# First attention layer: output weights fetched from ScalarE's queue, den steps one to an output unit, scale chain in four parts

## The chip, the cores and the metric

One NeuronCore of a Trainium2 chip runs the whole program. The metric is device time in microseconds (us) of one execution, lower is better. Each result below is a set of executions. One execution, of the set or beside it, is recorded by the hardware profiler, and its *span* is about 1.9 us shorter than its device time. Every execution also reports the mean clock that TensorE was granted (1.0 is full speed). "Fast" is what the records call all the runs compared.

## The reference, cut to what matters

Four residual layers on a 2048 x 1024 bf16 input: attention, gated unit, attention, gated unit, each behind a layer norm.

```python
# attention layer (1st and 3rd), H = 32 heads of 32
q, k, v = split(layernorm(x) @ wqkv)
pq, pk  = phi(q), phi(k)                  # phi(t) = t+1 if t>0 else exp(t), plus 1e-6
kv      = einsum("bhsd,bhse->bhde", pk, v)
den     = einsum("bhqd,bhd->bhq", pq, pk.sum(s)) + 1e-6
x       = x + (pq @ kv / den) @ wo
# gated layer (2nd and 4th)
x       = x + ((layernorm(x) @ w_gate) * (layernorm(x) @ w_up)) @ w_down
```

## The kernel before: what the change and the argument touch

The program is scheduled by hand: each engine executes its instructions in the order in which the Python code emits them. An attention layer goes: k units, key products (`xk`), twelve q units mixed with key products, a `kv` unit, four more q units mixed with eight key-value-output units (`kvo_unit`, the first users of `wo`), then 16 output units (`out_tile`). The first layer also does work for the second: it scans all gated-layer weights (`scans`, a Square with an accumulator on ScalarE), turns the sums into power-of-two scales (the scale chain), and prepares the first down weights (`dp`).

```python
wo = [ST[:]..., TX[:, 0:HEAD]...]        # the two halves of the output weights; ST, TX held normalised rows

def load_o():
    for n in range(2):
        nc.sync.dma_start(out=wo[n], in_=wo_v[:, :, n * NB:(n + 1) * NB])

def scale_pow(lo, hi):
    ps = mm_tile()
    nc.tensor.matmul(out=ps[:, lo:hi], lhsT=ones[:], rhs=partb[:, lo:hi], start=True, stop=True)
    nc.vector.tensor_scalar(out=part[:, lo:hi], in0=ps[:, lo:hi], scalar1=1e-30, ..., op0=ALU.max)
    nc.gpsimd.tensor_tensor(out=fac[:, lo:hi], in0=part[:, lo:hi], in1=mhalf[:, lo:hi], op=ALU.pow)

# den: multiply and sum of a q tile, or the division of a q tile and its transpose (a SyncE DMA).
# Steps are queued in `later`; flush() emits one.
def den_divide(t, pq, den):
    nc.vector.tensor_tensor(...)          # L479 in the profile
    tx(pq, t, t // TPG)                   # L308: transpose DMA, issued by SyncE

        for t in range(XT_):              # XT_ = 11
            pos = [-(-len(rest) * x // (XT_ - 1)) for x in (t, t + 1)]
            q_tile(t, li > 0, done=2 * (t < XT_ - 1))   # emits 2 queued den steps too
            do(rest[pos[0]:pos[1]])       # this unit's share of the remaining key products
            ...
            if t == XT_ - 3:
                load_o()
            scans((1, 2, 2, 2, 2, 2, 2, 2, 1, 0, 0)[t])
        ...
            job(18, lambda: scale_pow(2, 3))
            job(21, lambda: scale_bits(2, 3))
            ...
                job((22, 23, 26, 27)[i], f)       # dp: scale and sum down weights, store them (WD)
        ...
        for t in range(NT):               # 16 output units
            out_tile(t)                   # L510 matmuls, then VectorE's X add, L512
            if t < 3:
                flush()
                flush()
            do(jobs.get(2 * t, []))
            do(jobs.get(2 * t + 1, []))
```

## Time and profile before

| | before |
|---|---|
| device time, first 3 runs | 1499.6, 1494.09, 1496.38 us (median 1496.38) |
| profiled span | 1492.9 us |
| TensorE busy | 1482.9 us, 99% |
| all waits of TensorE in the table of waits | 7.0 us |

Engine names in the profile: PE is TensorE's matmuls, DVE VectorE, ACT ScalarE, POOL GpSimd, SP SyncE; a q after the name (SPq, ACTq) is that engine's instruction queue, where DMAs are issued. L500 is line 500 of that kernel.

The kernel before, the whole table of TensorE's waits: engine and line that waited, who ended the wait, total us, times, longest.

```profile
PE Q L510 <- DVE X L512: 1.4, 2, 1.0
PE Q L500 <- DMA TX<-in_A_wo_dram: 1.4, 1, 1.4
PE Q L181 <- DVE K L179: 1.2, 1, 1.2
PE Q L576 <- DVE TX L541: 0.9, 1, 0.9
PE Q L372 <- DMA XT<-ST: 0.8, 1, 0.8
PE Q L325 <- DVE TX L276: 0.7, 1, 0.7
PE Q L372 <- ACT XT L342: 0.4, 1, 0.4
PE Q L372 <- ACT XT L326: 0.2, 1, 0.2
```

Three of these lie where the change works: the output weights ("wait 1", L500), output units that wait for the X add ("wait 2", L510), and the second layer's first units waiting for a sum ("wait 3", L576).

The kernel before, SyncE's timeline: start us, duration us, engine and line, DMA.

```profile
148.64 14.39 SPq L308 DMA_TRANSPOSE XT<-W  x3
163.12 0.53 SPq L146 DMA_DIRECT2D ST<-in_A_wo_dram  x1
163.71 0.63 SPq L146 DMA_DIRECT2D TX<-in_A_wo_dram  x1
164.55 4.23 SPq L308 DMA_TRANSPOSE XT<-MX  x1
```

SyncE's queue stands at three transposes that wait for VectorE's divisions. The output weights sit behind them, though ST and TX came free when the last key product ended at about 155 us.

The kernel before, GpSimd's timeline, then ScalarE's; the bracket is the idle time before the instruction and what ended it.

```profile
224.66 0.55 POOL L238 TENSOR_TENSOR fac<-part,mhalf 128x1 f32<-128x1 f32 x1 [5.29 <-DVE part L237]
```

```profile
226.42 1.24 ACT L302 ACTIVATE ST<-X,of,rs 128x1024 bf16<-128x1024 bf16 x1 [4.85 <-POOL of L299]
```

GpSimd's power waits for TensorE's sum, and a norm's offset waits behind it in GpSimd's queue; ScalarE idles 4.85 us for that offset.

The kernel before, VectorE's timeline: the X adds of output units 4 to 6 (the first frees the pair of PSUM banks, TensorE's output memory, that unit 7 writes to), and the first sum of the second layer's input.

```profile
211.47 3.47 DVE L512 TENSOR_TENSOR X<-X,Q 128x1024 bf16<-128x1024 bf16 x3
...
244.79 1.23 DVE L541 TENSOR_TENSOR TX<-XT,XT 128x2048 f16<-128x2048 bf16 x1 [2.51 <-issue]
```

### The profile page before, as it was taken

Reading aid. Unit: us, or ns where it says so; the run is one execution under the profiler, and the core shown is the slowest. Engines: PE = TensorE matmul, PEld = TensorE weight load, DVE = VectorE, ACT = ScalarE, POOL = GpSimd, SP = SyncE. Lnnn points to the kernel's source line nnn. Section 1 sums busy time; section 2 is a strip of 40 time slices with the busy share of each in tenths; the row PEclk is TensorE's granted clock in tenths of the full one; section 3 lists DMA queues with packets and bytes.
Section 4 is the critical chain, followed back from the end, with each engine's and each line's share of the span. In section 5 each row is a group of like instructions: output and inputs, shape, how many; then the busy total and the mean of one; then the engine's idle time right before and its main releaser. Section 6 shows DMA issues by size and latency. Waiting matters only on the chain. (4 is left out here: it accounts for less than half of the span.)

```text
span 1492.9 us, 17625 instructions
## 1 busy us (share of the span) xinstructions
PE 1482.9 (99%) x6997; PEld 676.0 (45%) x6997; DVE 1008.1 (68%) x1426; ACT 707.9 (47%) x650; POOL 89.9 (6%) x206
## 2 busy tenths in 40 slices
PE   9999999999999999999999999999999999999999
PEld 3444444444444444444444445444444444444444
DVE  7856887888774577768285357767776845777532
ACT  4977695777601466540045337546554015656200
POOL 2121111000000000001020000200000100000000
DMA  7875875776656333336560015343332763333442
GB/s 212 226 242 166 217 143 160 220 204 204 215 174 172 85 87 91 95 110 211 148 170 1 14 29 127 64 110 94 95 90 99 220 181 99 85 85 85 148 168 86
DMA packets 269650, 202.74 MB, mean 136 GB/s; under 512 B 101760, under 2 KB 256896, under 8 KB 265984
## 3 DMA queue, kind: packets, MB, share of 16 engines
q1 hardware_dynamic: 265392, 186.81, 44.6%
q0 software_dynamic: 4032, 14.68, 3.2%
q8 instruction: 55, 0.90, 0.2%
q14 instruction: 27, 0.22, 0.0%
q10 hardware_dynamic: 144, 0.13, 0.0%
HBM read 160.43 MB, written 17.04 MB: 119 GB/s over the span
## 5 line engine op out<-in xcount | busy, mean ns | idle before, releaser
L576 PEld LDWEIGHTS <-K 128*128 128x128 f16 x3136 | 306.8, 98 | 371.1 <-DVE TX L541 1.4
L576 PE MATMUL Q<-XT,K 128*128 128x512 bf16 (+1 forms) x1792 | 405.7, 379 | 0.0
L871 PE MATMUL Q<-K,K 128*128 128x512 f16 (+2 forms) x1582 | 340.4, 377 | 0.0
L576 PE MATMUL Q<-TX,K 128*128 128x512 f16 x1344 | 308.4, 379 | 0.9 <-DVE TX L541 0.9
L538 ACT ACTIVATE K<-K,fac 128x2048 f16<-128x2048 bf16 x112 | 224.7, 2008 | 129.0 <-DMA K<-in_B_w_gate_dram 129.0
L871 PEld LDWEIGHTS <-K 128*128 128x128 f16 x1582 | 154.3, 98 | 184.5
L541 DVE TENSOR_TENSOR K<-K 128x1024 f16<-128x1024 f16 (+1 forms) x244 | 157.1, 666 | 102.8 <-ACT K L538 100.8
L355 ACT ACTIVATE W<-Q 128x1024 bf16<-128x1024 f32 (+1 forms) x68 | 65.7, 968 | 145.6 <-PE Q L372 145.6
L541 DVE TENSOR_TENSOR W<-MX,Q 128x1024 f16<-128x1024 f32 x88 | 107.4, 1220 | 37.3 <-PE Q L576 18.4
L596 ACT COPY MX<-Q 128x1024 f32<-128x1024 f32 x60 | 60.8, 1013 | 122.6 <-PE Q L576 109.3
L372 PE MATMUL Q<-K,XT 128*128 128x512 bf16 x512 | 113.5, 379 | 1.4 <-DMA XT<-ST 0.8
L372 PE MATMUL Q<-K,K 128*128 128x512 bf16 x512 | 114.1, 379 | 0.0
L541 DVE TENSOR_TENSOR W<-W,Q 128x1024 f16<-128x1024 f32 x80 | 97.6, 1220 | 17.9 <-PE Q L576 13.5
L596 ACT COPY W<-Q 128x1024 f32<-128x1024 f32 x52 | 52.7, 1013 | 91.9 <-PE Q L576 79.2
L541 DVE TENSOR_TENSOR K<-K,K 128x512 f16<-128x512 f16 (+1 forms) x148 | 87.7, 597 | 4.2
L360 DVE TENSOR_SCALAR W<-W 128x1024 bf16<-128x1024 bf16 (+1 forms) x68 | 27.8, 408 | 85.2 <-ACT W L355 85.1
L372 PEld LDWEIGHTS <-K 128*128 128x128 bf16 x512 | 50.0, 98 | 61.4 <-issue 1.7
L372 PEld LDWEIGHTS <-XT 128*128 128x128 bf16 x512 | 49.4, 98 | 61.2 <-DMA XT<-ST 1.3
L580 DVE TENSOR_TENSOR K<-W 128x512 f16<-128x512 f16 x168 | 71.3, 425 | 5.7
L221 ACT ACTIVATE K<-K 128x2048 bf16<-128x2048 bf16 x36 | 68.6, 1908 | 7.7 <-DMA K<-in_B_w_down_dram 6.9
L258 DVE BATCH_NORM_STATS2 st<-X 128x6 f32<-128x512 bf16 x104 | 65.8, 674 | 2.6 <-DMA X<-in_A_x_dram 2.6
L885 DVE SCALAR_TENSOR_TENSOR W<-Q,kap,X 128x1024 f32<-128x1024 f32 x16 | 20.5, 1284 | 66.2 <-PE Q L871 66.2
(125 smaller groups left out, 1155.8 us busy)
## 6 DMA issues: line engine op xcount, KB each, us to landing
K<-WD SPq DMA_DIRECT2D x28, 1792.0 KB, 7.4
K<-in_B_w_gate_dram SPq DMA_DIRECT2D x70, 512.0 KB, 4.2
K<-in_B_w_up_dram SPq DMA_DIRECT2D x56, 512.0 KB, 5.2
K<-in_A_wqkv_dram SPq DMA_DIRECT2D x10, 1024.0 KB, 7.7
K<-in_B_w_up_dram POOLq DMA_DIRECT2D x11, 512.0 KB, 5.7
K<-in_B_w_down_dram POOLq DMA_DIRECT2D x11, 512.0 KB, 9.4
K<-in_B_w_down_dram SPq DMA_DIRECT2D x10, 512.0 KB, 5.4
WD<-K SPq DMA_DIRECT2D x10, 512.0 KB, 3.0
```

What stands on the lines that cost most here:

```text
L221: nc.scalar.activation(out=scan_buf[i], in_=scan_buf[i], func=ACT.Square, accum_out=acc[:, m, c:c + 1])
L258: nc.vector.bn_stats(out=stat[t][0][:, c, :], in_=X[:, t, c * NB:(c + 1) * NB])
L355: nc.scalar.activation(out=e, in_=ps, func=ACT.Exp)
L360: nc.vector.tensor_scalar(out=e, in0=e, scalar1=1.0, scalar2=1e-6, op0=ALU.min, op1=ALU.add)
L372: nc.tensor.matmul(out=ps, lhsT=xt[:, k, tl * P:(tl + 1) * P], rhs=w[:, k, :], start=(k == 0), stop=(k == KD - 1))
L538: nc.scalar.activation(out=b.bitcast(F16), in_=b, func=ACT.Copy, scale=fac[:, m:m + 1])
L541: eng.tensor_tensor(out=o, in0=a, in1=b, op=op)
L576: nc.tensor.matmul(out=pair[:, m, :], lhsT=stationary(n, p, m, k), rhs=moving[p][:, k, :], start=(p in (1, 2, 5) and k == 0), stop=(k == K ...
L580: nc.vector.tensor_tensor(out=hA[i][:, u, :], in0=gu[:, 0, :], in1=gu[:, 1, :], op=ALU.mult)
L596: nc.scalar.copy(out=snaps[u, p], in_=a)
L871: nc.tensor.matmul(out=ps_[:, lo:hi], lhsT=act[:, u, j * P:(j + 1) * P], rhs=w[:, u, lo:hi], start=(p in (1, 2, 5) and u == 0), stop=(u == ...
L885: stt(out=o, in0=ps_, scalar=kap[:, 0:1], in1=x, op0=ALU.mult, op1=ALU.add)
```

## The change

The intent is to take the last small waits out of the end of the first layer: fetch the output weights as soon as their buffers are free and from a queue that is not standing, spread VectorE's den steps so that X adds come sooner, and keep GpSimd's power from holding up a norm. The whole diff but for hunk headers:

```diff
     def load_o():
         for n in range(2):
-            nc.sync.dma_start(out=wo[n], in_=wo_v[:, :, n * NB:(n + 1) * NB])
+            nc.scalar.dma_start(out=wo[n], in_=wo_v[:, :, n * NB:(n + 1) * NB])
...                                                       # in scale_pow, before the power:
+
+    def scale_root(lo, hi):
         nc.gpsimd.tensor_tensor(out=fac[:, lo:hi], ..., op=ALU.pow)
...
             pos = [-(-len(rest) * x // (XT_ - 1)) for x in (t, t + 1)]
+            xks = rest[pos[0]:pos[1]]
+            if t == XT_ - 2:
+                do(xks)
+                xks = []
+                load_o()
             q_tile(t, li > 0, done=2 * (t < XT_ - 1))
-            do(rest[pos[0]:pos[1]])
+            do(xks)
...
                 scale_pow(0, 2)
+                scale_root(0, 2)
...
-            if t == XT_ - 3:
-                load_o()
...
-            job(21, lambda: scale_bits(2, 3))
+            job(20, lambda: scale_root(2, 3))
+            job(22, lambda: scale_bits(2, 3))
...
-                job((22, 23, 26, 27)[i], f)
+                job((23, 24, 26, 27)[i], f)
...
             out_tile(t)
-            if t < 3:
-                flush()
+            if t < 6:
                 flush()
```

## The prediction

> **What bounds the kernel.** TensorE. The page gives it 1482.9 of 1492.9 us busy (99%), clock 1.0. Its table of waits lists only 7.0 us in all, of which four, 3.7 us, lie in the stages that this change touches:
> 1. 1.42 us at 170.6 us: the second half of the output weights (TX<-in_A_wo_dram) has not landed for the first key-value-output unit, first layer.
> 2. 1.05 us at 211.7: output unit 7 waits for a PSUM pair that VectorE's X add frees, first layer; 0.36 us at 951 is the same in the third layer.
> 3. 0.89 us at 247.4: the second layer's first units wait for a VectorE sum of the transposed input (TX).
> The rest are start-up waits, untouched. So the change cannot win more than about 3.7 us (0.25%).
>
> **What it does.** The instruction lists show TensorE's order *identical* before and after: with five key products left, the share of the tenth q unit was already empty, so "last key product ahead" is a no-op here. What moves:
> - Output weights. SyncE issues them at 163.1/163.7 us, stuck behind three transposes that wait for VectorE (148.6 to 163.1, timeline); landing takes 5.8 to 8.3 us. ScalarE would issue after its weight scan ending 159.4. Two issues cost 0.53+0.63 us; if that holds on ScalarE, the next Exp slips to about 160.5, still ready for VectorE at 161.65. Landing by about 169 (estimate from the 8.3 us), before 170.4. Wait 1 goes. The Trainium skill (DMA: Bandwidth & Descriptors, "Issuing engines are not separate DMA queues") says another issuing engine saves only issue time; here what is saved is the in-order queue wait, 3 to 4 us. In the third layer the key product gates it: no effect.
> - Den steps. Six steps over six output units instead of three. X add 4, which frees output unit 7's pair, came behind all of them; now one 1.22 us divide comes after it. VectorE has almost no idle time between 179 and 215, so the add comes about 1.13 us earlier. But removing wait 1 moves TensorE 1.42 us up, so it asks earlier. VectorE's 1.27 us gap at 175.4 (waiting for ScalarE, itself behind TensorE) should close in step. I expect 0 to 0.4 us of wait 2 left; nothing in the third layer.
> - Scale chain. GpSimd's power at 224.66 sits 5.29 us waiting for TensorE's sum, in order ahead of a norm's offset: ScalarE's apply at 226.42 idles 4.85 us. Two jobs later unblocks it. Normalisations 6 and 7 also go ahead of the down-weight sums, and their transposes ahead of the WD stores (before: 238.75, after stores). I expect them to land about 2 us sooner or better: wait 3 goes.
>
> Nothing arithmetic is added; only four DMA issues (about 2.3 us in all) move to ScalarE, 47% busy.
>
> **Sum.** 1.42+1.05+0.36+0.89 = 3.7 us at most, about 3.4 expected: 1496.4 to **1493.0 us**, range 1489.5 to 1496.5 (the three runs of before spread 5.5 us, more than the gain). Chances: faster by over 2% 0.005, within 2% 0.99, slower by over 2% 0.005.
>
> **What would show it.** TensorE's waits fall from 7.0 to about 3.5 us, with no line for in_A_wo and none, or under 0.5 us, for X adds; TensorE busy unchanged at 1483; ScalarE's 4.85 us idle before its normalise gone; span about 1489.5.
>
> **What would make it wrong.** The issues block ScalarE longer than on SyncE, so Exp and then TensorE wait; VectorE stays the limit and gives wait 1 back at output unit 7; GpSimd's power, now later, holds the scaling that the next layer needs; run-to-run spread hides it all.

## The result, and the profile after

| | before | after |
|---|---|---|
| device time | 1494.09, 1496.38, 1499.14, 1499.6 us; median 1497.76 | 1490.3, 1490.67, 1490.81, 1490.83 us; median 1490.74 |
| ratio of fast runs | | 0.9956, 95% interval 0.9935 to 0.9977 |
| profiled span | 1492.9 us | 1489.0 us |
| TensorE busy | 1482.9 us | 1482.4 us |
| span less TensorE busy | 10.0 us | 6.6 us |

A ratio is the mean time of one kernel's fast runs over the mean of the other's of the same rounds, so it is not quite the ratio of the medians quoted. The interval is clear of 1, so the change gains about 0.4%, some 6.6 us. The traces differ by only 3.9 us (1492.9 to 1489.0). Most of the other 2.7 us is the draw: the profiled execution of before took 1494.76 us, 2.5 us less than the mean of its set (1497.30 us), while that of after, 1490.81 us, lies at the mean of its own (1490.65 us). So what had to be explained is why before is often slower than its trace, and spreads more (5.5 us against 0.5).

The kernel after, the whole table of TensorE's waits.

```profile
PE Q L181 <- DVE K L179: 1.2, 1, 1.2
PE Q L374 <- DMA XT<-ST: 0.7, 1, 0.7
PE Q L327 <- DVE TX L278: 0.7, 1, 0.7
PE Q L374 <- ACT XT L344: 0.4, 1, 0.4
PE Q L398 <- DVE K L366: 0.3, 1, 0.3
PE Q L374 <- ACT XT L328: 0.2, 1, 0.2
PE Q L374 <- DMA K<-in_A_wqkv_dram: 0.2, 1, 0.2
```

Waits 1, 2 and 3 are gone; 3.7 us remain, all before 92 us.

The kernel after, ScalarE's timeline around the issue.

```profile
158.02 1.91 ACT L221 ACTIVATE W<-W 128x2048 bf16<-128x2048 bf16 x1 [0.90 <-DMA W<-in_B_w_down_dram]
158.07 0.38 ACTq L146 DMA_DIRECT2D ST<-in_A_wo_dram  x1
158.49 0.59 ACTq L146 DMA_DIRECT2D TX<-in_A_wo_dram  x1
159.84 0.19 ACT L221 ACTIVATION_READ_ACCUMULATOR W<-W 128x1 f32 x1
159.93 1.00 ACT L357 ACTIVATE W<-Q 128x1024 bf16<-128x1024 f32 x1
```

The two issues run while the scan's Square executes: the queue has run ahead of the compute. They come 5 us earlier than in the kernel before and cost ScalarE's compute nothing; the Exp (L357) follows right behind the scan.

The kernel after, VectorE's timeline: X add of output unit 4, and the first sum of the second layer's input.

```profile
208.29 1.21 DVE L514 TENSOR_TENSOR X<-X,Q 128x1024 bf16<-128x1024 bf16 x1
...
239.34 1.22 DVE L543 TENSOR_TENSOR TX<-XT,XT 128x2048 f16<-128x2048 bf16 x1
```

The X add comes 3.2 us earlier than before (211.47) and the sum 5.5 us earlier (244.79). TensorE's own second-layer start moved by only 2.4 us (243.84 to 241.45), so both waits turned into slack.

The kernel after, GpSimd's power and ScalarE's normalise.

```profile
223.51 0.57 POOL L240 TENSOR_TENSOR fac<-part,mhalf 128x1 f32<-128x1 f32 x1
```

```profile
219.65 2.55 ACT L304 ACTIVATE ST<-X,of,rs 128x1024 bf16<-128x1024 bf16 x2
```

Neither has a bracket: the power no longer waits, and the fourth normalise follows the third at once.

### The profile page after: what moved, and what is told of

It reads as the page before. It is cut to its first block, busy times and chain, and to the rows that moved or that the text cites. A ratio compares the mean times of both kernels' runs of the same rounds, so it can differ in the third digit from the quotient of the medians.

```text
span 1489.0 us, 17622 instructions
## 1 busy us (share of the span) xinstructions
PE 1482.4 (100%) x6997; PEld 675.9 (45%) x6997; DVE 1007.3 (68%) x1426; ACT 707.8 (48%) x650; POOL 89.5 (6%) x206
## 4 chain that ended last, share of the span: by engine, by line
PE 94%; DMA 2%; ACT 2%; DVE 1%; issue 1%; SPq 0%; POOL 0%; ACTq 0%; DVEq 0%; POOLq 0%
PE Q L578 45%; PE Q L877 23%; PE Q L374 11%; PE Q L512 7%; PE Q L398 6%; DMA K<-in_A_wqkv_dram 1%; ACT K L221 1%; ACT W L357 1%; DMA X<-in_A_x_dram 1%; PE Q L492 0%; PE Q L502 0%; DVE st L260 0%; DMA K<-in_B_w_gate_dram 0%; ACT K L287 0%; SPq L138 0%
## 5 line engine op out<-in xcount | busy, mean ns | idle before, releaser
L357 ACT ACTIVATE W<-Q 128x1024 bf16<-128x1024 f32 (+1 forms) x68 | 65.7, 968 | 145.6 <-PE Q L374 145.5
```

Source lines behind the costliest of these rows:

```text
L357: nc.scalar.activation(out=e, in_=ps, func=ACT.Exp)
```

## The experiments

Twelve runs were made, all correct. The first eight came in two groups of four on two chips, each with 11 runs of the kernel before beside them (medians 1496.13 and 1498.64 us, so compare within a group). The last four shared 10 runs of it (median 1495.31 us).

### One part alone, and the issue moved without changing engines

`wo_only`: before with this edit.

```diff
-            nc.sync.dma_start(out=wo[n], ...
+            nc.scalar.dma_start(out=wo[n], ...
```

> Before, with only the output weights issued from ScalarE. Theory W (the missing 2.7 us between the profile's 3.9 us and the timed 6.6 us is wait 1, which is longer than 1.42 us in the slow runs of before): timed gain 3.5 to 5 us and a spread under 1.5 us; in the profile no wait on in_A_wo, wait 2 (unit 7 on the X add) 1.0 to 1.4 us because the den steps are unmoved, wait 3 still about 0.9 us. Rival T (the spread comes from wait 3, the late transposes): timed gain about 1.3 us, spread still about 5 us. Rival V (VectorE gives wait 1 back): span gain under 0.5 us and wait 2 grown to about 2.4 us.

Measured: 1493.67 us median (1492.37 to 1498.07), ratio 0.9984 (0.9967 to 1.0001), about 2.4 us, with an interval that just includes no effect. The issue came at 154.7 us and wait 1 was gone. Wait 2 was 0.8 us in two waits of 0.4, where 1.0 to 1.4 had been expected; wait 3 stayed at 0.9 us. Rival V is refuted: wait 2 shrank instead of growing. Theory W's gain of 3.5 us and its narrow spread did not appear in these six runs.

`den_only`: before with one flush for each of six output units (`if t < 6: flush()`).

> Before, with only one den step per output unit. Wait 2 gone in both layers (1.05 and 0.36 us), waits 1 and 3 unchanged (1.4 and 0.9 us): span gain 1.0 to 1.5 us. Theory W and rival T both say the spread of before stays, about 5 us, and so a timed gain of 1 to 2 us with a wide interval. If the spread goes, it was VectorE's.

Measured: 1497.22 us median (1494.84 to 1505.5), ratio 1.0011 (0.9988 to 1.0034). The X-add waits were gone in both layers, as expected (wait 1 was 0.70 us, not the expected 1.4), but no gain shows in the time, and the spread stayed wide. Its trace happens to hold a wait of 1.84 us for another weight load at 91.7 us, upstream of the change, so its span (1493.3 us) cannot be compared to a microsecond.

`scale_only`: before with `scale_root` split off and the jobs at 20, 22, 23 and 24.

> Before, with only the scale chain in four parts and its jobs moved. ScalarE's 4.85 us idle before its fourth normalise gone, transposes of tiles 6 and 7 ahead of the WD stores, wait 3 gone: span gain 0.8 to 1.0 us. Theory W: spread stays at about 5 us. Rival T: spread falls under 1.5 us and the timed gain is 3 us or more.

Measured: 1494.34 us median (1493.04 to 1501.17), ratio 0.9991 (0.9971 to 1.001). Wait 3 was gone and ScalarE's fourth normalise no longer idled; wait 1 stood at 1.3 us. The spread stayed (8.1 us), so rival T, that the late transposes make it, falls.

`sp_early`: before, with the key product really moved in the first layer, and SyncE still the issuer.

```diff
+            xks = rest[pos[0]:pos[1]]
+            if li == 0 and t == XT_ - 3:
+                do(xks)
+                xks = []
+                load_o()
             q_tile(t, li > 0, done=2 * (t < XT_ - 1))
-            do(rest[pos[0]:pos[1]])
+            do(xks)
...
-            if t == XT_ - 3:
+            if li > 0 and t == XT_ - 3:
                 load_o()
```

> Before, with the last key product of the first layer really put ahead of the ninth q unit, and the output weights issued there, still by SyncE, ahead of the third waiting transpose. If the in-order wait is the cause, and not which engine issues: issue at 152 to 157 us instead of 163.1, no wait on in_A_wo, and a timed gain and a spread like wo_only's within 1 us. If ScalarE's own queue is what helps: wait 1 stays near 1.4 us.

Measured: 1494.04 us median (1492.87 to 1496.8), ratio 0.9984, the same as `wo_only`. The kernel `sp_early`, the lines of the DMA issue (duration ns min/median/max, first and last start us):

```profile
L146 SPq DMA_DIRECT2D ST<-in_A_wo_dram x2: 532/532/533, 153.9 to 895.4; - x2
L146 SPq DMA_DIRECT2D TX<-in_A_wo_dram x2: 626/628/630, 154.4 to 896.0; - x2
```

Issued at 153.9 us by SyncE, the weights are in time as well: TensorE's table of waits has no line for them. As far as these runs resolve, what matters is when the fetch is issued, not which engine issues it. That agrees with the Trainium skill ("DMA: Bandwidth & Descriptors", section "Issuing engines are not separate DMA queues"), which says that another issuing engine saves only the time of the issue. The expectation missed on the spread: 3.9 us, not within 1 us of `wo_only`'s 5.7.

### The changed kernel again, and with one part undone

> The changed kernel once more, against before on one chip. If its narrow spread of the first four runs (0.5 us) is the change's doing: spread under 1.5 us again, median 1490 to 1491.5, gain 5 to 7 us. If those four were a lucky draw: spread 3 to 6 us like every other kernel's so far, and a gain near the profile's 3.9 us.

Measured: 1491.3 us median (1490.15 to 1493.37), ratio 0.9958 (0.9935 to 0.998), about 6.3 us. The gain repeats. The spread of 3.2 us is neither the 0.5 us of the first runs nor that of before (1493.79 to 1504.05 in the same rounds). Its trace, which is its slowest run, has no wait from 162 us on; it lost 1.70 us to another weight load at 91.6 us and 0.82 us to VectorE at 161 us. Neither comes from the moved fetch: the second follows a weight scan whose data came 2.21 us late, at 156.24 us, and the output weights were issued at 159.33 us.

`no_wo`: after, with `nc.sync` again in `load_o`.

> The changed kernel, but SyncE issues the output weights as before. Wait on in_A_wo back at 1.2 to 1.5 us, no other wait; 1.0 to 1.5 us slower than after_again in the span. Theory W: over 3 us slower when timed.

Measured: 1494.65 us median (1492.15 to 1499.23), ratio 0.9982. Against `after_again` that is 0.0024 of the time, about 3.6 us (0.5 to 6.7, a 95% estimate from the twelve runs), and the runs spread 7.1 us again: the timed part of theory W holds. But its trace does not show the expected wait; wait 1 is 0.19 us there because TensorE was already late. So that the 3.6 us are wait 1 is not shown. The kernel `no_wo`, TensorE's timeline:

```profile
160.97 5.30 PE L374 MATMUL Q<-K,K 128*128 128x512 bf16 x16 [2.48 <-DVE MX L366]
```

TensorE paused 2.48 us, and then 16 matmuls took 5.30 us where the same line's 16 take 3.61 us elsewhere. This was the first sight of a second cost: after a pause TensorE runs slower. The granted clock was 0.50 from 161.63 us on, for 3.41 us. The pause itself came from a weight scan whose data was late (ScalarE idled 3.99 us for it, and the Exp behind it in the queue was late); it starts before the output weights are issued in that kernel (166.2 us), so when they are issued does not explain it. `after_again`'s 0.82 us is the same pause in small.

`no_den`: after, with two flushes in each of three output units.

> The changed kernel with the den steps two to an output unit again. X-add wait of 0.35 to 0.4 us in each of the two attention layers back (up to 1 us in the first where a transpose lands late), nothing else: 0.7 to 1.5 us slower than after_again in the span.

Measured: 1491.78 us median (1491.0 to 1495.11), ratio 0.9962, about 0.6 us worse than `after_again`, which these runs do not resolve (plus or minus 1.8 us, estimated from the twelve). The kernel `no_den`, TensorE's waits:

```profile
PE Q L512 <- DVE X L514: 0.8, 2, 0.4
```

The expected 0.38 us in each attention layer is back and nothing else.

`no_scale`: after, with the old `scale_pow` and the old job places.

> The changed kernel with the old scale chain and job places. ScalarE idles 4 to 5 us behind GpSimd's power again, wait 3 back at 0.85 to 0.9 us: 0.9 us slower than after_again in the span.

Measured: 1491.26 us median (1491.09 to 1492.97), ratio 0.9958, no slower than `after_again`. The kernel `no_scale`, TensorE's timeline:

```profile
245.38 3.63 PE L576 MATMUL Q<-TX,K 128*128 128x512 f16 x16 [0.86 <-DVE TX L541]
```

Wait 3 is back at 0.86 us (ScalarE's idle before the fourth normalise at 3.2 us, less than expected). The timed runs do not show it; `after_again` lost as much elsewhere, and six runs with a spread of 2 to 3 us do not settle 0.9 us.

### How large wait 1 can be, and what it costs

`wo_late`: before, with the issue behind one more transpose.

```diff
-            if t == XT_ - 3:
+            if t == (XT_ - 1 if first_A else XT_ - 3):
                 load_o()
```

> Before with the first layer's output weights issued one transpose later still on SyncE (two q units later in the program). Issue at 166 to 169 us, landing 8 us later, so wait 1 of 4 to 7 us. Theory C (a TensorE pause of more than about 2.5 us is followed by microseconds at a lower granted clock, as the 2.48 us pause of no_wo was, and so costs more than itself): granted clock under 0.9 for some microseconds just after the wait, 16 matmuls there taking over 4.5 us instead of 3.6, clock of every run 0.999 or less, and the time up by the longer wait plus 1 to 2 us. Rival: clock stays 1.0 and only the wait is paid.

Measured: 1504.93 us median (1504.59 to 1510.02), ratio 1.0072 (1.0058 to 1.0086); clock 0.995 to 0.997 in all six runs. The issue came at 165.9 us, 2.8 us later than before, yet the second half took 14.8 us to land instead of 8.3. The kernel `wo_late`, TensorE's timeline:

```profile
171.69 0.38 PE L500 MATMUL Q<-ST,W 128*128 128x512 bf16 x1 [1.00 <-DMA ST<-in_A_wo_dram]
181.38 0.58 PE L500 MATMUL Q<-TX,W 128*128 128x512 bf16 x1 [9.31 <-DMA TX<-in_A_wo_dram]
181.76 3.06 PE L372 MATMUL Q<-K,K 128*128 128x512 bf16 x8
```

The waits were 10.3 us, more than the 4 to 7 expected, because the landing stretched too. Theory C holds, and its rival falls: the granted clock was 0.50 from 173.88 to 184.12 us, that is from inside the pause to 2.7 us past its end, and 8 matmuls that take 1.89 us elsewhere took 3.06 us. The span is 10.0 us longer than in the first trace of before, of which the longer wait is 8.9.

`before_a`, `before_b`, `before_c`: the kernel before, unchanged, to catch a slow execution.

> The kernel before, unchanged, to catch one of its slow executions in a trace (8 of 22 showed a clock below 1.0). If the time is over 1497 us: theory S says a late weight-scan transfer holds ScalarE, hence an Exp, VectorE, the transposes and the issue of the output weights; wait 1 over 2 us, or a wait on VectorE at about 161 us, with a lower clock after it. If it is under 1496 us: waits as in the first profile.

> A second draw of the kernel before, unchanged, with the same expectation as before_a: over 1497 us, wait 1 over 2 us or a wait on VectorE at about 161 us and a lower clock after it; under 1496 us, the waits of the first profile.

> A third draw of the kernel before, unchanged, with the same expectation as before_a: over 1497 us, wait 1 over 2 us or a wait on VectorE at about 161 us and a lower clock after it; under 1496 us, the waits of the first profile.

(The "8 of 22" in the first of these is a slip: the runs listed for the two groups show 2 and 5 of 11, that is 7 of 22.)

Measured: 1495.77, 1502.37 and 1493.97 us. The first and the third have waits 1 and 2 as in the first profile, but larger (1.64 and 1.83 us) and smaller (0.73 and 0.37 us). The second is the slow execution looked for. The kernel `before_b`, TensorE's timeline:

```profile
174.60 0.59 PE L500 MATMUL Q<-TX,W 128*128 128x512 bf16 x1 [3.92 <-DMA TX<-in_A_wo_dram]
174.98 3.23 PE L372 MATMUL Q<-K,K 128*128 128x512 bf16 x8
...
212.87 3.61 PE L510 MATMUL Q<-K,XT 128*128 128x512 bf16 x15 [0.56 <-DVE X L512]
218.80 5.21 PE L510 MATMUL Q<-K,XT 128*128 128x512 bf16 x16 [2.31 <-DVE X L512]
```

Wait 1 was 3.92 us, and wait 2 was 0.56 + 2.31 us. Behind each long pause the matmuls are slow: 3.23 us for 8, 5.21 us for 16. The granted clock was 0.50 for 3.41 us each time, from 174.27 and from 218.64 us. The kernel `before_b`, VectorE's waits between 160 and 215 us, the largest two:

```profile
DVE W L360 <- ACT W L355: 5.5, 2, 5.3
DVE MX L362 <- DMA K<-MX: 2.6, 1, 2.6
```

The second of these lines in the first trace of before, then in `before_a`:

```profile
DVE MX L362 <- DMA K<-MX: 0.8, 1, 0.8
DVE MX L362 <- DMA K<-MX: 1.4, 1, 1.4
```

VectorE waits for a transpose to land that frees a buffer, and its lateness becomes wait 2. The traces agree on this: with 0.8, 1.4 and 2.6 us of it, wait 2 in the first layer was 1.05, 1.83 and 2.87 us. `before_c` and `scale_only`, without the line, had 0.37 and 0.38 us, though their fetch was as late. No trace with the early fetch has the line.

Was the issue late, as theory S said? No: 163.16 and 163.74 us, as in the first trace. The landing was, 10.8 us instead of 8.3 for the second half. Theory S falls. The kernel `before_b`, stretches of 4 us: length, then the busy us of PE, its weight loads, DVE, ACT and POOL, TensorE's granted clock, DMA share (packets' times over the time of 16 engines, so it can pass 1), GB/s.

```profile
158.00:162.00 4.00, 4.00 (x28) 2.04 (x26) 3.86 (x6) 2.89 (x4) 0.00 (x0) 1.00 0.01 2
166.00:170.00 4.00, 4.00 (x20) 1.85 (x19) 3.68 (x10) 1.22 (x2) 3.43 (x5) 1.00 0.98 339
170.00:174.00 4.00, 0.68 (x4) 0.20 (x2) 3.56 (x6) 0.80 (x1) 0.96 (x2) 1.00 1.27 158
174.00:178.00 4.00, 3.40 (x9) 1.27 (x9) 1.43 (x2) 1.11 (x1) 0.00 (x0) 0.57 1.48 61
```

The kernel after, the same view:

```profile
158.00:162.00 4.00, 4.00 (x23) 1.86 (x22) 3.86 (x6) 2.91 (x3) 0.00 (x0) 1.00 0.67 217
162.00:166.00 4.00, 4.00 (x68) 3.75 (x66) 3.88 (x5) 1.02 (x1) 0.00 (x0) 1.00 1.21 339
166.00:170.00 4.00, 4.00 (x21) 1.77 (x19) 3.66 (x9) 0.89 (x1) 3.29 (x5) 1.00 0.92 224
170.00:174.00 4.00, 4.00 (x20) 1.85 (x19) 3.21 (x6) 2.83 (x4) 1.11 (x2) 1.00 1.12 348
```

Before, the DMA engines are idle from 158 to 162 us (2 GB/s), because the fetch stands in SyncE's queue. It is then issued just ahead of five down-weight loads from GpSimd (from 167.3 us) and of a gate and an up load from SyncE. After, the fetch fills the idle stretch. Ahead of the collision it also relieves its neighbours. The gate load, us from issue to landing, in the first trace of before and after:

```profile
K<-in_B_w_gate_dram SPq DMA_DIRECT2D x1, 512.0 KB, 16.3
K<-in_B_w_gate_dram SPq DMA_DIRECT2D x1, 512.0 KB, 4.6
```

It took 14.1 to 21.6 us in the eight traces with the late fetch and 4.2 to 4.6 us in the six with the early one. The down-weight loads do not part so cleanly: their median is 18.4 us in `before_b`, 12.6 us in the first trace of before and 7.9 us after, but also 7.8 us in `before_c` and `den_only`, whose fetch was late.

This sums up the slow run. Against `before_c` (span 1492.1 us, wait 1 of 0.73, wait 2 of 0.37 us in the first layer), `before_b` (1500.5 us) has 3.2 us more of wait 1, 2.5 us more of wait 2, and 1.3 + 1.6 us of slow matmuls behind the two pauses. That is 8.6 us, against the 8.4 us between the two spans; small differences in the start-up make up the rest.

### The clock over all runs

| output weights issued | kernels | runs with clock below 1.0 |
|---|---|---|
| by SyncE at about 163 us or later, as before | before (35 runs), den_only, scale_only, no_wo (6 each) | 19 of 53 |
| at 153 to 160 us, by either engine | after (10 runs), wo_only, sp_early, no_den, no_scale (6 each) | 1 of 34 |
| one transpose later | wo_late | 6 of 6 |

The 35 runs of before are those whose clock is listed in these experiments (11, 11 and 10 beside them, and the three looks). Within each chip the picture is the same: 7 of 23 against 1 of 12 on the first, 12 of 30 against 0 of 18 on the other (the 4 first runs of after apart). One stretch of 3.41 us at half clock lowers the mean clock of a run by about 0.001 (an estimate: half of 3.41 us over 1495 us), so 0.999 stands for about one and 0.998 for two, as in `before_b`. So when the fetch is issued largely decides whether a run gets a pause long enough to lower the clock, though not alone, and which pause it was is known only for the traced runs: `no_wo`'s trace has a low clock from another pause, and `wo_only` spread 5.7 us with one low-clock run of six.

## Why the prediction was right, and where it was not

- **No-op.** "The instruction lists show TensorE's order *identical*" held: TensorE's busy time is 1482.4 against 1482.9 us, and nothing of the gain comes from the key product.
- **Wait 1.** It went as predicted, and `sp_early` shows the reason to be the in-order queue. The predicted small cost, "the next Exp slips to about 160.5", did not occur: the issues ran under the scan's Square and the Exp began at 159.93 us.
- **Wait 2.** "0 to 0.4 us of wait 2 left" was right at 0. The den steps are worth the 0.38 us in each of the two layers that `no_den` shows. What the traces of before had above that (1.05, 1.83 and 2.87 us in the first layer) is VectorE's wait for a late-landing transpose (0.8, 1.4 and 2.6 us), seen only with the late fetch, and not in every trace of it. The prediction had put wait 2 down to VectorE's order alone.
- **Wait 3.** Gone as predicted. The sum came 5.5 us sooner, of which 2.4 us is TensorE's own shift, so "about 2 us sooner or better" was modest. The timed runs do not resolve what it is worth.
- **Remaining waits.** "From 7.0 to about 3.5 us", and a span of "about 1489.5": measured 3.7 us and 1489.0 us.
- **The term that was mis-sized.** "1.42+1.05+0.36+0.89 = 3.7 us at most" was no ceiling. It summed the waits of one fast trace. Over four traces of before, wait 1 was 1.42, 1.64, 3.92 and 0.73 us, and wait 2 in the first layer 1.05, 1.83, 2.87 and 0.37 us, and pauses over 2.3 us cost up to 1.7 us more through the clock. That is the likely place where the timed gain of 6.6 us found what the trace pair's 3.9 us lacked; the timed runs themselves have no traces. The gain was nearly twice the 3.4 us expected. The time still fell into the range, 1489.5 to 1496.5 us, because the range had been made wide for the spread, and that part is luck. The prediction named "the three runs of before spread 5.5 us, more than the gain" as noise that might hide the result; by the traces and the clock table, much of that spread comes from the very waits being removed.

What stays open: why the same program, issuing at the same time, moved 158 and then 61 GB/s in `before_b` where the first trace moved 230 and 328 in the same stretches; which pauses the untraced runs of `no_wo` had (four of its six show a low clock, one of them traced); and what the scale chain is worth in time, since `scale_only` (0.9991, against before) and `no_scale` (0.9958, as `after_again`) show no effect beyond their intervals. Nor do the timed parts add up to the whole of 6.3 us: alone they gave 2.4, -1.6 and 1.3 us, and undone they cost 3.6, 0.6 and 0 us, each to within about 1 to 4 us. No version tried beats the changed kernel by more than the spread.

## What to carry to other kernels

A wait on a DMA in one trace is a sample, not a constant: when runs spread more than the waits that you see, suspect a landing time that varies, and look at several traces before you call the sum of waits a ceiling. An early-ready fetch must not stand in an in-order DMA queue behind transposes that wait for compute; put it where its data is first free, in a stretch where the DMA engines are idle, from whichever queue gets there. On a TensorE-bound kernel a long pause can cost more than itself: here pauses of 2.31 us and more brought at least 3.41 us at half clock, and those of up to 1.84 us did not.

## What the Trainium skill lacked or had wrong

- "TensorE: Matmul & The Clock Gate", section "HAM oscillation — how this bites in real kernels", gives the rule "no PE-idle gaps >~3.4µs". Here gaps of 2.31 us (`before_b`) and 2.48 us (`no_wo`) already brought a clock of 0.50 for 3.41 us, while 1.83 us (`before_a`) and 1.84 us (`den_only`) did not. The page's half clock agrees with the run: 0.50 was granted from 173.88 to 184.12 us in `wo_late`, around the end of its 9.31 us pause.
- The same section's example has about 1.67 us of throttled time for each gap, half of it lost. One episode here lasted 3.41 us and lost 1.3 to 1.7 us on top of the pause (8 matmuls 3.23 instead of 1.89 us, 16 matmuls 5.21 or 5.30 instead of 3.61 us).
- "DMA: Bandwidth & Descriptors", section "Issuing engines are not separate DMA queues", says that another issuing engine saves only the issue time, "usually small relative to the DMA itself". It leaves out the time that a ready DMA stands behind one that waits in the same queue: 5 us between the issue on SyncE (163.12 us) and on ScalarE (158.07 us), and a wait of 0.73 to 3.92 us in the four traces of before that the early issue takes away.
- No page read for this says outright that a DMA issued from ScalarE's queue runs while ScalarE computes: 0.38 and 0.59 us of issue under a 1.91 us Square.
- "Perfetto Trace Analysis", section "DMA Instruction — HWDGE (DVE, Sync)", says that data movement lies outside the profiled window of the issue. The runs agree: the same issue of 0.61 to 0.63 us had landings of 8.3, 10.8 and 14.8 us. The page gives no hint of how far landings of one DMA can vary from run to run.
